# A linear-attention, expert-layer and feed-forward kernel: the attention's inverse products over 128 rows, and the constants and tables around them packed

## The chip, the cores and the metric

The kernel runs on one core of a Trainium2 chip. The core has five engines that work side by side: TensorE (PE, matrix products; its weight loads are listed apart as PEld), VectorE (DVE), ScalarE (ACT), GpSimd (POOL) and SyncE (SP, which here only issues transfers). Sixteen DMA engines move data between the chip's memory and the core's on-chip memory, SBUF; PE writes to a second on-chip memory, PSUM. [...] The metric is the time of one execution in microseconds (us) of the device; less is better.

## The reference

Three parts follow each other. A recurrence over 768 steps for 4 x 8 heads, each with a 40 x 40 state; a layer of eight experts, of which each of 3072 tokens takes two; and a feed-forward layer with leaky rectifier. All that is changed lies in the recurrence:

```python
def _attn_ref(r, k, v, w, a, b):
    state = np.zeros((B, H, D, D)); y = np.zeros_like(r)
    for t in range(S):
        ...
        y[:, :, t] = np.einsum('bhd,bhde->bhe', rt, state)
        Sa = np.einsum('bhde,bhe->bhd', state, at)
        state_decay = state * wt[:, :, None, :] - np.einsum('bhd,bhe->bhde', Sa, bt)
        state = state_decay + np.einsum('bhd,bhe->bhde', vt, kt)
```

## The kernel before

**Chunks.** The 768 steps are cut into 12 chunks of 64. Within a chunk the steps' mutual dependence is solved by blocks: a chunk falls into two blocks (blk) of 32 steps, each of two halves (h) of 16, and for each 16 steps the inverse of a small triangular matrix is kept. The 32 heads are split into two bands (f = 0, 1) of 16 each, and the 16 into four groups g of four (z).

**The scan over a chunk.** For each group g, `c_x` (lines 163 to 175) gathers right sides: products of the state S with aT and of VU with g, in line 167, go to PSUM tile bk, and two copies by ACT (line 175) put them into the tile x[g]. Only 16 rows of x are written for each band: rows 0 to 15 and 32 to 47 for an even chunk, 64 to 79 and 96 to 111 for an odd one (p0 is 64 for odd chunks). `c_u` (lines 176 to 182) multiplies them with the inverse: line 180 runs eight products of 32 output rows and 40 columns, from 64 rows of TT (the weights) and 64 rows of x:

```python
for f in range(2): nc.tensor.matmul(pu[32*f:32*f+n,z],TT[p0:p0+64,16*h:16*h+n,2*(4*g+z)+blk],x[p0:p0+64,z,f],...)
```

The profile shows each such product as two, 3072 in all. The weights of one product are 32 elements of TT, each 32 elements (128 bytes) behind the one before. ACT (line 182) copies the result into VU, from which the next `c_x` reads. After four rounds `c_s` (line 183) brings the state forward: products of kb with VU in line 189, then DVE in lines 191 and 194. The four groups and neighbouring chunks overlap on PE; `y_s` and `y_y` (lines 203 to 223: lines 207, 215 and 220 on PE) make the output of a chunk, and `logits` (line 340) the first step of the expert layer.

**Preparing a chunk.** `wq` (line 76) runs twice for each chunk and makes running products of the decays by two scans on DVE: Dt (line 82, backwards, with the constant tile cd, which holds 4096 in every 64th column) and Et (line 88, forwards, with ce, whose every 64th column is set in line 87). POOL multiplies aT by Et (line 93). `sta` and `stk_` stack operands, and a transposing DMA in line 107 turns each of them (at, kbt; rt, ut and sd are further ones); `ks` (line 122) multiplies kbt with at in line 129, and stores a part, ns, to memory as nd (line 134). For two chunks at a time, `t_load` (line 137) fetches nd into N (line 139) and sets the tile T to unit matrices, `t_step` (line 143) eliminates in 15 steps (two operations of line 148 each, on POOL; on DVE for chunk 0), and `t_fin` (line 149) transposes T by DVE into one of two tiles TT (line 151). Chunks 0 and 1 are alone, so that only one half of T and TT is filled for them.

**Tiles.** T is 128 x 32 x 32, of which 32 matrices of 16 x 16 use the left 16 of each 32 columns. The tile tm holds products of a step. TT is 128 x 48 x 32; its rows 16 to 31 are cleared at the start (line 250), since a product of half h reads 32 rows of it from row 16h.

**Order.** `run` (line 232) lists all steps with a due time (`at(k, f, ...)`) and emits them by it. The program is then placed by the framework's own scheduler, which works with estimated durations, so the order on an engine is fixed when the program is built, and can change over a long stretch when one instruction changes. All loads, stores and transposing DMAs of this stage stand in one queue, SP's.

Of the kernel before, what the change touches and what calls it, by code (L numbers as in the profile page):

```python
# [7 lines left out]
F32 = mybir.dt.float32  # L8
# [4 lines left out]
ALU = mybir.AluOpType  # L13
# [16 lines left out]
class Attn:  # L30
# [7 lines left out]
    def consts(s,tp):  # L38
        nc=s.nc; cp=s.cp; V=nc.vector; G=nc.gpsimd;

        s.S=cp.tile([128,16,120],F32,name="S"); G.memset(s.S,0.0)
        s.ss=cp.tile([128,16,128],F16,name="ss"); V.memset(s.ss,0.0)
        s.x=[cp.tile([128,4,2,40],F32,name=f"x{i}") for i in range(4)]
        for t in s.x: G.memset(t,0.0)
# [31 lines left out]
    def wq(s,c,q):  # L76
# [3 lines left out]
        def rv(t): b=t[:,n-1:n]; return bass.AP(tensor=b.tensor,offset=b.offset,ap=[b.ap[0],[-1,n]])  # L80
        w=s.K['w',c,q]; ws=w[:,1:513].rearrange("p (a b)->p a b",b=64); w0=s.w0[:,c,is_]
        V.tensor_tensor_scan(rv(f2(Dt)),rv(w[:,2:514]),rv(f2(s.cd)),0.0,ALU.mult,ALU.add)  # L82
        W4=wp.tile([104,8],F32,name="W4",bufs=2)
        V.tensor_copy(ws[:,:,0],w0); V.memset(ws[:,:,63],0.0)
        V.tensor_tensor(W4,w0,Dt[:,:,0],ALU.mult)
        V.tensor_scalar(w0,W4,2.0**-12,None,op0=ALU.mult)
        V.reciprocal(W4,W4); V.tensor_scalar(s.ce[:,:,0],W4,2.0**15,None,op0=ALU.mult)
        V.tensor_tensor_scan(f2(Et),w[:,0:512],f2(s.ce),0.0,ALU.mult,ALU.add)  # L88
        v=lambda t: t.rearrange("p z (o x)->p z o x",o=2)[:,:,:,0:40]
# [47 lines left out]
    def t_load(s,c):  # L137
        nc=s.nc; wk=s.wk; p=s.tp(c)
        nc.sync.dma_start(out=s.N[p].rearrange("p a b->p (a b)"),in_=s.K[c]['nd'][p])
        e=nc.gpsimd; e.memset(s.blk(c,s.T,0,[32,16],[1,16]),0.0); e.memset(s.blk(c,s.T,0,[33,16]),1.0)  # L140
    def blk(s,c,t,off,*d):
        x=t.rearrange("p a b->p (a b)")[s.tp(c),0:1]; return bass.AP(tensor=x.tensor,offset=x.offset+off,ap=[x.ap[0],[512+16*(t is s.N),2]]+[list(z) for z in d])
    def t_step(s,c,j):
        nc=s.nc; n,m=15-j,j+1; te=s.cfg['te0' if c==0 else 'te']
        e=nc.vector if te=='V' else nc.gpsimd
        t=s.tm[s.tp(c),0:2*n*m].rearrange("p (o a b)->p o a b",o=2,b=m)
        nd,T0,T1=s.blk(c,s.N,33*j+1,[1,n],[0,m]),s.blk(c,s.T,32*j,[0,n],[1,m]),s.blk(c,s.T,32*m,[32,n],[1,m])
        e.tensor_tensor(t,nd,T0,ALU.mult); e.tensor_tensor(T1,T1,t,ALU.subtract)
    def t_fin(s,c):
        s.nT+=1; TT=s.TT[s.nT%2]; p=s.tp(c); f2=lambda x: x.rearrange("p a b->p (a b)")  # L150
        for i in range(2): s.tlast=s.nc.vector.transpose(f2(TT[p,32*i:32*i+16]),f2(s.T[p,16*i:16*i+16]))
        for i in s.tg[c]: s.K[i]['TT']=TT
# [10 lines left out]
    def c_x(s,c,g,blk,h):  # L163
        nc=s.nc; K=s.K[c]; aT=s.aT[c%s.cfg['NA']]; VU=s.VU[c%2]; p0=64*(c%2); cs=slice(32*blk+16*h,32*blk+16*h+16); st=[True]*2
        px=s.bk[g]
        def mm(f,c0,n,l,r):
            q=64+32*f; nc.tensor.matmul(px[q:q+16,c0:c0+n],l,r,start=st[f],stop=True,skip_group_check=True); st[f]=False  # L167
        if c:
            for j in range(2):
                for f in range(2): i=4*g+2*j+f; mm(f,80*j,80,aT[:,i,cs],s.S[:,i,0:80])  # L170
        for z in range(4):
            for f in range(2): mm(f,40*z,40,K['g',f][:,4*g+z,cs],VU[:,f,4*g+z,:])
        x=s.x[g]
        for f in range(2):
            nc.scalar.activation(x[p0+32*f:p0+32*f+16,:,f],px[64+32*f:80+32*f,0:160].rearrange("p (z d)->p z d",d=40),AF.Copy,scale=-0.125)  # L175
    def c_u(s,c,g,blk,h):
        nc=s.nc; TT=s.K[c]['TT']; VU=s.VU[c%2]; p0=64*(c%2); x=s.x[g]; n=32
        pu=s.bk[g][:,0:160].rearrange("p (a d)->p a d",a=4)
        for z in range(4):
            for f in range(2): nc.tensor.matmul(pu[32*f:32*f+n,z],TT[p0:p0+64,16*h:16*h+n,2*(4*g+z)+blk],x[p0:p0+64,z,f],start=h==0 and z==0,stop=True,skip_group_check=True)  # L180
        for f in range(2):
            q=64-64*f+32*blk; nc.scalar.activation(VU[q:q+n,f,4*g:4*g+4],pu[32*f:32*f+n],AF.Copy)  # L182
# [49 lines left out]
    def run(s):  # L232
        nc=s.nc; F=s.cfg; s.st=s.P("ast"); s.wk=s.P("awk")
        s.pre=ExitStack(); s.wp=s.pre.enter_context(s.tc.tile_pool(name="awp",bufs=1)); s.ctx.enter_context(s.pre)
        V=nc.vector
        zero=lambda t: (nc.gpsimd if t.dtype==F32 else V).memset(t,0.0)
        s.w0=s.wk.tile([104,NCH,16],F32,name="w0"); nc.sync.dma_start(out=s.w0.rearrange("p a b->p (a b)"),in_=s.h['w0'])
        s.cd=s.wp.tile([104,8,64],F32,name="cd"); s.ce=s.wp.tile([104,8,64],F32,name="ce")
        zero(s.cd); zero(s.ce); V.memset(s.cd[:,:,63:64],4096.0)
        s.aT=[s.st.tile([128,16,64],F32,name=f"aT{i}") for i in range(F['NA'])]  # L240
# [5 lines left out]
        for t in s.VU: zero(t)  # L246
        s.T=s.wk.tile([128,32,32],F32,name="T",bufs=1); zero(s.T)
        s.N=s.wk.tile([128,32,32],F32,name="N",bufs=1); s.tm=s.wk.tile([128,272],F32,name="tmp",bufs=1)
        s.TT=[s.st.tile([128,48,32],F32,name=f"TT{i}") for i in range(2)]; s.nT=0
        for t in s.TT: zero(t[:,16:32])  # L250
        s.bk=[s.ps.tile([128,512],F32,name=f"bk{g}",bufs=1) for g in range(4)]
# [613 lines left out]
```

## Time and profile before

| | us |
|---|---|
| median of 3 runs (1504.52 to 1516.42) | 1512.85 |
| the profiled execution | 1518.96 |
| its span, from the first to the last instruction | 1517.2 |

| engine | busy us | share of the span | instructions |
|---|---|---|---|
| PE | 1207.4 | 80% | 15975 |
| PEld | 909.3 | 60% | 15975 |
| DVE | 892.2 | 59% | 2029 |
| ACT | 641.7 | 42% | 1535 |
| POOL | 482.7 | 32% | 559 |

The profile records one execution. A busy time is the time in which at least one instruction of the engine ran; PE's products overlap each other, so their starts and not their durations show the pace, and the ends are modelled. The chain of waits is followed back from the last instruction, at each step to what released it. [...] In the rows, `L180 PE MATMUL bk<-x,TT 64*32 64x40 f32 x16` is sixteen products of line 180 that write bk from x and TT, with 64 rows and 32 columns of weights, and 64 x 40 elements that run through.

### The profile page before, as it was taken

The page shows a single profiled execution, that of the slowest core. Times are in us where ns is not written, and L with a number is a line of the kernel's source. Part 1 is how long each engine was busy: PE and PEld are TensorE (multiplying, and loading weights), DVE is VectorE, ACT ScalarE, POOL GpSimd, SP SyncE. Part 2 cuts the span into 40 slices and gives each one's busy share as a digit, 9 for nine tenths or more (in the row PEclk, how much of TensorE's full clock was granted, in tenths as well). Part 3 has the DMA queues.
Part 4 walks back from the last instruction along what each step waited for, and adds up shares of the span by engine and source line. Part 5 has one row for each costly group of instructions (what it writes and reads, how often), then busy time and mean ns, then how long its engine had stood idle before and what let it go on. Part 6 is the DMA issues. An engine that isn't in the chain of part 4 may idle for free.

```text
span 1517.2 us, 37921 instructions
## 1 busy us (share of the span) xinstructions
PE 1207.4 (80%) x15975; PEld 909.3 (60%) x15975; DVE 892.2 (59%) x2029; ACT 641.7 (42%) x1535; POOL 482.7 (32%) x559
## 2 busy tenths in 40 slices
PE   1348877879788879627877978779895899999998
PEld 0237766768677768515646746547675565555555
DVE  6798655765666589674644554869732764442321
ACT  1247556565666755332422223325221544433432
POOL 7365414224152343132402102030003525423422
PEclk9999688885878977758999989889998899999999
DMA  7779787877867664559637766465312522110000
GB/s 216 142 139 196 139 157 145 151 128 157 157 129 142 120 141 107 104 176 177 165 107 204 205 208 180 121 194 138 119 44 82 109 66 48 35 36 18 18 18 21
DMA packets 305939, 188.17 MB, mean 124 GB/s; under 512 B 260894, under 2 KB 276355, under 8 KB 304891
## 3 DMA queue, kind: packets, MB, share of 16 engines
q1 hardware_dynamic: 293103, 156.91, 46.7%
q0 software_dynamic: 10368, 16.84, 4.4%
q10 hardware_dynamic: 2288, 11.90, 2.3%
q8 instruction: 127, 2.08, 0.6%
q14 instruction: 53, 0.43, 0.1%
HBM read 105.24 MB, written 23.18 MB: 85 GB/s over the span
## 4 chain that ended last, share of the span: by engine, by line
PE 49%; DVE 21%; DMA 18%; issue 4%; POOL 3%; ACT 3%; SPq 2%; another core or an unknown queue 1%; DVEq 0%; POOLq 0%; ACTq 0%
PE ph L661 10%; PE po L671 9%; PE po L565 9%; PE ph L551 7%; DMA wf<-w 7%; PE bk L167 5%; DMA kbt<-stk 3%; PE bk L180 3%; DVE l L520 2%; DVE S L194 2%; DVE kb L99 2%; DVE Dt L82 1%; DVE wam L510 1%; DVE Et L88 1%; DMA N<-nd 1%
## 5 line engine op out<-in xcount | busy, mean ns | idle before, releaser
L551 PE MATMUL ph<-xT,h 128*128 128x372 f16 (+2 forms) x680 | 151.6, 353 | 83.7 <-DVE gl L554 56.3
L553 ACT ACTIVATE gh<-ph 128x372 f16<-128x372 f32 (+2 forms) x136 | 68.1, 509 | 260.9 <-PE ph L551 221.6
L529 POOL DMA_INDIRECT xr<-xs,ix x56 | 82.9, 1480 | 254.8 <-DMA xT<-xr 234.5
L175 ACT ACTIVATE x<-bk 16x160 f32<-16x160 f32 x384 | 113.7, 296 | 94.8 <-PE bk L167 87.6
L551 PEld LDWEIGHTS <-h 128*128 128x128 f16 x680 | 68.5, 101 | 129.6 <-issue 93.5
L665 POOL TENSOR_TENSOR gl<-hc,gh 128x512 f16<-128x512 f32 x80 | 91.9, 1157 | 146.7 <-ACT gh L664 146.6
L565 PE MATMUL po<-h,gh 128*124 128x320 f16 x448 | 135.4, 303 | 0.6 <-ACT y L567 0.4
L565 PE MATMUL po<-l,gh 128*124 128x320 f16 x448 | 134.7, 303 | 0.0
L565 PE MATMUL po<-h,gl 128*124 128x320 f16 x448 | 134.2, 304 | 0.0
L180 PE MATMUL bk<-x,TT 64*32 64x40 f32 x3072 | 130.7, 244 | 2.5 <-issue 1.7
L661 PE MATMUL ph<-xT,wih 128*128 128x512 f16 (+2 forms) x560 | 125.2, 354 | 7.8 <-DVE hc L663 4.5
L167 PE MATMUL bk<-S,aT 128*16 128x80 f32 x1408 | 105.5, 276 | 31.0 <-DVE S L194 19.4
L565 PEld LDWEIGHTS <-gh 128*124 128x124 f16 x896 | 122.4, 137 | 10.2 <-issue 0.9
L182 ACT ACTIVATE VU<-bk 32x160 f32<-32x160 f32 x384 | 112.4, 293 | 35.9 <-PE bk L180 27.2
L167 PE MATMUL bk<-VU,g 128*16 128x40 f32 x3072 | 126.0, 230 | 1.7 <-ACT VU L182 1.7
L663 DVE SCALAR_TENSOR_TENSOR hc<-ph,hc 128x512 f32<-128x512 f32 (+2 forms) x112 | 68.4, 612 | 98.2 <-ACT hc L662 93.3
L180 PEld LDWEIGHTS bk<-x,TT 64*32 64x32 f32 x3072 | 109.7, 156 | 16.8 <-issue 5.0
L671 PE MATMUL po<-woh,gh 128*128 128x320 f16 x384 | 114.1, 301 | 5.0 <-issue 3.7
L671 PE MATMUL po<-wol,gh 128*128 128x320 f16 x384 | 113.8, 301 | 0.0
L639 POOL DMA_INDIRECT yy<-yd,slot x48 | 48.6, 1013 | 204.6 <-DMA yd<-y 157.5
L664 ACT ACTIVATE gh<-hc 128x512 f16<-128x512 f32 (+2 forms) x112 | 62.5, 566 | 119.5 <-PE po L671 66.6
L671 PE MATMUL po<-woh,gl 128*128 128x320 f16 x384 | 109.4, 301 | 0.1
(286 smaller groups left out, 2504.0 us busy)
## 6 DMA issues: line engine op xcount, KB each, us to landing
wf<-w SPq DMA_DIRECT2D x24, 512.0 KB
w<-wi SPq DMA_DIRECT2D x16, 768.0 KB
wf<-w SPq DMA_DIRECT2D x32, 320.0 KB
w<-wo SPq DMA_DIRECT2D x16, 640.0 KB
kb<-kb SPq DMA_DIRECT2D x24, 320.0 KB
yd<-y ACTq DMA_DIRECT2D x7, 1085.0 KB
w<-wz SPq DMA_DIRECT2D x24, 208.8 KB
aa<-aa SPq DMA_DIRECT2D x12, 320.0 KB
```

Source lines behind the costliest of these rows:

```text
L167: q=64+32*f; nc.tensor.matmul(px[q:q+16,c0:c0+n],l,r,start=st[f],stop=True,skip_group_check=True); st[f]=False
L175: nc.scalar.activation(x[p0+32*f:p0+32*f+16,:,f],px[64+32*f:80+32*f,0:160].rearrange("p (z d)->p z d",d=40),AF.Copy,scale=-0.125)
L180: for f in range(2): nc.tensor.matmul(pu[32*f:32*f+n,z],TT[p0:p0+64,16*h:16*h+n,2*(4*g+z)+blk],x[p0:p0+64,z,f],start=h==0 and z==0,stop=Tr ...
L182: q=64-64*f+32*blk; nc.scalar.activation(VU[q:q+n,f,4*g:4*g+4],pu[32*f:32*f+n],AF.Copy)
L529: c=e*NJ+j; nc.gpsimd.indirect_dma_start(out=xr[0:PT,j],out_offset=None,in_=s.xs,in_offset=bass.IndirectOffsetOnAxis(ap=s.ix[0:PT,c:c+1],a ...
L551: for n,(t,k,i) in enumerate(ps): nc.tensor.matmul(ph[:,0:N],w(t,k,f),xT[:,j0:j1,i,0:PT],start=n==0,stop=n==7)
L553: nc.scalar.activation(o,ph[:,0:N],AF.Relu)
L565: nc.tensor.matmul(po[0:PT,0:DM],a[:,f,c],b[:,DM*f:DM*f+DM],start=n==0,stop=n==23); n+=1
L661: for n,(t,k,i) in enumerate(ps): nc.tensor.matmul(ph[:,0:N],w(t,k,f),xT[:,b0:b1,i,:],start=n==0,stop=n==7)
L663: nc.vector.scalar_tensor_tensor(c,ph[:,0:N],0.01,c,ALU.mult,ALU.max)
L665: (nc.vector if g<2 else nc.gpsimd).tensor_tensor(gl[:,f,0:N],c,gh[:,f,0:N],ALU.subtract)
L671: nc.tensor.matmul(po[:,0:DM],a[:,f,128*(b-b0):128*(b-b0)+128],bb[:,f,:],start=n==0,stop=n==47); n+=1
```

## The change

Five edits go together.

1. There are eight tiles x in place of four: an odd chunk has its own. As all of them are cleared at the start and `c_x` writes the same rows as before, the rows of the other parity stay zero. The product of line 180 (182 now) runs over all 128 rows of TT and x.
2. Both tiles TT are cleared as a whole at the start.
3. T is packed: 33 x 16 columns in place of 32 x 32, so a row of a matrix stands 16 elements behind the one before, not 32. The transposition in `t_fin` still reads 32 columns for each row, of which the second 16 are now the next row; they end in rows of TT that meet zero rows of x.
4. The tile tm has 128 columns in place of 272.
5. The constant tile cd goes. ce has 520 columns and serves both scans: ahead of each Dt scan a memset on DVE puts 4096 into columns 64, 128, ... 512, and the Dt scan reads ce from column 1 on; ahead of the Et scan columns 0, 64, ... 448 are written as before.

```diff
@@ -40,7 +40,7 @@
-        s.x=[cp.tile([128,4,2,40],F32,name=f"x{i}") for i in range(4)]
+        s.x=[cp.tile([128,4,2,40],F32,name=f"x{i}") for i in range(8)]
         for t in s.x: G.memset(t,0.0)
@@ -79,13 +79,14 @@
-        V.tensor_tensor_scan(rv(f2(Dt)),rv(w[:,2:514]),rv(f2(s.cd)),0.0,ALU.mult,ALU.add)
+        ce=s.ce[:,0:512].rearrange('p (a b)->p a b',b=64)[:,:,0]; V.memset(bass.AP(tensor=s.ce[:,64:65].tensor,offset=s.ce[:,64:65].offset,ap=[s.ce[:,64:65].ap[0],[64,8]]),4096.0)
+        V.tensor_tensor_scan(rv(f2(Dt)),rv(w[:,2:514]),rv(s.ce[:,1:513]),0.0,ALU.mult,ALU.add)
         ...
-        V.reciprocal(W4,W4); V.tensor_scalar(s.ce[:,:,0],W4,2.0**15,None,op0=ALU.mult)
-        V.tensor_tensor_scan(f2(Et),w[:,0:512],f2(s.ce),0.0,ALU.mult,ALU.add)
+        V.reciprocal(W4,W4); V.tensor_scalar(ce,W4,2.0**15,None,op0=ALU.mult)
+        V.tensor_tensor_scan(f2(Et),w[:,0:512],s.ce[:,0:512],0.0,ALU.mult,ALU.add)
@@ -137,18 +138,19 @@
-        e=nc.gpsimd; e.memset(s.blk(c,s.T,0,[32,16],[1,16]),0.0); e.memset(s.blk(c,s.T,0,[33,16]),1.0)
+        e=nc.gpsimd; e.memset(s.blk(c,s.T,0,[16,16],[1,16]),0.0); e.memset(s.blk(c,s.T,0,[17,16]),1.0)
...
-        nd,T0,T1=s.blk(c,s.N,33*j+1,[1,n],[0,m]),s.blk(c,s.T,32*j,[0,n],[1,m]),s.blk(c,s.T,32*m,[32,n],[1,m])
+        nd,T0,T1=s.blk(c,s.N,33*j+1,[1,n],[0,m]),s.blk(c,s.T,16*j,[0,n],[1,m]),s.blk(c,s.T,16*m,[16,n],[1,m])
...
-        for i in range(2): s.tlast=s.nc.vector.transpose(f2(TT[p,32*i:32*i+16]),f2(s.T[p,16*i:16*i+16]))
+        for i in range(2):
+            t=s.T[p,16*i:16*i+1]; s.tlast=s.nc.vector.transpose(TT[p,32*i:32*i+16],bass.AP(tensor=t.tensor,offset=t.offset,ap=[t.ap[0],[16,16],[1,32]]))
@@ -170,14 +172,14 @@
-        x=s.x[g]
+        x=s.x[4*(c%2)+g]
...
-            for f in range(2): nc.tensor.matmul(pu[32*f:32*f+n,z],TT[p0:p0+64,16*h:16*h+n,2*(4*g+z)+blk],x[p0:p0+64,z,f],start=h==0 and z==0,stop=True,skip_group_check=True)
+            for f in range(2): nc.tensor.matmul(pu[32*f:32*f+n,z],TT[:,16*h:16*h+n,2*(4*g+z)+blk],x[:,z,f],start=h==0 and z==0,stop=True,skip_group_check=True)
@@ -235,8 +237,8 @@
-        s.cd=s.wp.tile([104,8,64],F32,name="cd"); s.ce=s.wp.tile([104,8,64],F32,name="ce")
-        zero(s.cd); zero(s.ce); V.memset(s.cd[:,:,63:64],4096.0)
+        s.ce=s.wp.tile([104,520],F32,name="ce")
+        zero(s.ce)
@@ -244,10 +246,10 @@
-        s.T=s.wk.tile([128,32,32],F32,name="T",bufs=1); zero(s.T)
-        s.N=s.wk.tile([128,32,32],F32,name="N",bufs=1); s.tm=s.wk.tile([128,272],F32,name="tmp",bufs=1)
+        s.T=s.wk.tile([128,33,16],F32,name="T",bufs=1); zero(s.T)
+        s.N=s.wk.tile([128,32,32],F32,name="N",bufs=1); s.tm=s.wk.tile([128,128],F32,name="tmp",bufs=1)
         s.TT=[s.st.tile([128,48,32],F32,name=f"TT{i}") for i in range(2)]; s.nT=0
-        for t in s.TT: zero(t[:,16:32])
+        for t in s.TT: zero(t)
```

The change also moves instructions on every engine, since the scheduler places the program anew. Up to line 82 the lines keep their numbers; line 167 becomes 169, 180 becomes 182, 220 becomes 222. Three places follow, before and after.

On PE, at the place that the profile before shows at 432 us: products of the scan (L167: right sides, L180: with the inverse, L189: state) and of the output (L220). The numbers behind bk, x and TT are those of buffers; an `x8` is the eight products of one `c_u`. Before:

```order
L167 MATMUL bk_195<-VU_96,g 16x40 x4
L180 MATMUL bk_196<-x_90,TT_190 32x40 x8
L180 MATMUL bk_193<-x_87,TT_190 32x40 x3
L220 MATMUL yy<-kb,s_6103 32x40 x16
L180 MATMUL bk_193<-x_87,TT_190 32x40 x5
L180 MATMUL bk_194<-x_88,TT_190 32x40 x8
L180 MATMUL bk_195<-x_89,TT_190 32x40 x8
L189 MATMUL bk_196<-VU_95,kb 40x40 x8
```

After:

```order
L169 MATMUL bk_200<-VU_104,g 16x40 x4
L182 MATMUL bk_201<-x_90,TT_195 32x40 x8
L182 MATMUL bk_198<-x_91,TT_195 32x40 x3
L222 MATMUL yy<-kb,s_6130 32x40 x16
L182 MATMUL bk_198<-x_91,TT_195 32x40 x5
L182 MATMUL bk_199<-x_92,TT_195 32x40 x8
L182 MATMUL bk_200<-x_93,TT_195 32x40 x8
L191 MATMUL bk_201<-VU_103,kb 40x40 x8
```

The sequence is the same here; line 182 reads tiles of even (x_87 to x_90) and of odd chunks (x_91 to x_94), so two chunks meet within one run of products, before as after.

In SP's queue, around the transposing DMA of at that the profile before shows at 188 us (aa is a load that at is made from, nd a store, VU, rr, w and kb loads). Before:

```order
L66 DMA w<-wz 104x514
L73 DMA aa<-aa 128x640
L74 DMA aT_161<-at 40x1024 x2
L66 DMA w<-wz 104x514
L107 DMA_TRANSPOSE at<-stk_176 128x16x128
L134 DMA nd<-ns 64x16x32
L107 DMA_TRANSPOSE kbt<-stk_177 128x16x128
L107 DMA_TRANSPOSE ut<-us 128x16x128
L161 DMA VU_96<-vv 64x640 x2
L155 DMA rr<-rr 128x640
L107 DMA_TRANSPOSE kbt<-stk_175 128x16x128
L134 DMA nd<-ns 64x16x32
```

After:

```order
L74 DMA aT_166<-at 40x1024 x2
L66 DMA w<-wz 104x514
L135 DMA nd<-ns 64x16x32
L108 DMA_TRANSPOSE ut<-us 128x16x128
L163 DMA VU_104<-vv 64x640 x2
L73 DMA aa<-aa 128x640
L108 DMA_TRANSPOSE at<-stk_181 128x16x128
L108 DMA_TRANSPOSE kbt<-stk_182 128x16x128
L66 DMA w<-wz 104x514
L157 DMA rr<-rr 128x640
L108 DMA_TRANSPOSE kbt<-stk_180 128x16x128
L135 DMA nd<-ns 64x16x32
```

The load of aa and the transposes of at and of the first kbt stood ahead of the transpose of ut and the loads of VU, and stand behind them now.

On POOL, at the end of the memsets of the start-up. Before:

```order
L236 MEMSET aT_163 32x1024 x2
L236 MEMSET aT_164 32x1024 x2
L236 MEMSET TT_189 128x512
L236 MEMSET TT_190 128x512
L93 TENSOR_TENSOR aT_160<-aT_160,Et 104x512 x2
L104 TENSOR_TENSOR stk_176<-aa,stk_176 128x16x40
```

After:

```order
L238 MEMSET aT_168 32x1024 x2
L238 MEMSET aT_169 32x1024 x2
L238 MEMSET TT_194 128x1536
L238 MEMSET TT_195 128x1536
L94 TENSOR_TENSOR aT_165<-aT_165,Et 104x512 x2
L105 TENSOR_TENSOR stk_181<-aa,stk_181 128x16x40
```

The two memsets of TT stand at the same place, between those of aT and the first product aT times Et, with 1536 columns in place of 512.

## Rows read from the trace of the kernel before

**Rows 1.** Busy time by stretch (from:to, length, each engine in us, granted clock, DMA share, GB/s).

```profile
98.00:634.00 536.00, 443.75 (x11065) 387.77 (x11067) 368.51 (x913) 325.55 (x953) 196.75 (x307) 0.81 0.73 141
367.10:367.90 0.80, 0.80 (x22) 0.71 (x22) 0.80 (x1) 0.60 (x3) 0.00 (x0) 0.50 0.47 98
432.30:435.10 2.80, 2.80 (x112) 2.65 (x109) 1.28 (x3) 2.07 (x6) 0.93 (x1) 1.00 1.15 188
```

**Rows 2.** The chain of waits from 98 to 634 us, share of it by line.

```profile
by line: PE bk L167 13.4%; DMA kbt<-stk 7.8%; PE bk L180 7.8%; issue 5.4%; DVE S L194 4.6%; DVE kb L99 3.3%; DMA ut<-us 2.7%; DMA nd<-ns 2.5%; DMA N<-nd 2.3%; DVE Dt L82 2.3%; PE pt L95 2.0%; DMA kb<-kb 1.9%; DVE stk L106 1.9%; PE sc L129 1
```

**Rows 3.** Page, costliest groups: L180 products, busy us, mean ns, idle before.

```profile
L180 PE MATMUL bk<-x,TT 64*32 64x40 f32 x3072 | 130.7, 244 | 2.5 <-issue 1.7
```

**Rows 4.** Timeline of PE near 432 us: start us, busy us, engine, line, operation, count.

```profile
432.02 0.34 PE L167 MATMUL bk<-VU,g 128*16 128x40 f32 x8
432.29 0.74 PE L180 MATMUL bk<-x,TT 64*32 64x40 f32 x22
432.96 0.49 PE L220 MATMUL yy<-kb,s 128*32 128x40 f32 x32
433.38 1.54 PE L180 MATMUL bk<-x,TT 64*32 64x40 f32 x42
434.85 0.53 PE L189 MATMUL bk<-VU,kb 128*40 128x40 f32 x16
```

**Rows 5.** One line each: duration of one in ns (min/median/max), first and last start.

```profile
L180 PEld LDWEIGHTS bk<-x,TT x3072: 128/158/173, 98.4 to 633.1; 64*32 64x32 f32 x192
L180 PE MATMUL bk<-x,TT x3072: 208/235/288, 98.4 to 633.2; 64*32 64x40 f32 x192
L220 PEld LDWEIGHTS yy<-kb,s x1536: 105/113/178, 139.9 to 648.1; 128*32 128x32 f32 x192
L220 PE MATMUL yy<-kb,s x1536: 199/207/277, 139.9 to 648.1; 128*32 128x40 f32 x192
```

**Rows 6.** Timeline of PE near 512 us, two lines of 128 rows.

```profile
511.80 0.35 PE L167 MATMUL bk<-VU,g 128*16 128x40 f32 x10
511.95 0.23 PE L220 MATMUL yy<-kb,s 128*32 128x40 f32 x2
```

**Rows 7.** Timeline of PE near 367 us, at half the clock.

```profile
366.41 0.75 PE L167 MATMUL bk<-VU,g 128*16 128x40 f32 x16
367.08 0.76 PE L180 MATMUL bk<-x,TT 64*32 64x40 f32 x16
367.78 0.45 PE L167 MATMUL bk<-S,aT 128*16 128x80 f32 x4
```

**Rows 8.** Timeline of PE near 508 us, L180 of two chunks in a run.

```profile
508.38 0.97 PE L180 MATMUL bk<-x,TT 64*32 64x40 f32 x32
```

**Rows 9.** The chain in the start-up: start us, us, what.

```profile
24.84 0.99 POOL TT L236 x2
25.83 1.24 POOL aT L93
```

**Rows 10.** POOL to 30 us by line: count, busy us, mean ns, idle before.

```profile
L236 POOL MEMSET aT<- 32x1024 f32 x10 | 9.4, 944 | 5.3 <-DVE bad L798 4.9
L41 POOL MEMSET S<- 128x1920 f32 x1 | 1.7, 1697 | 0.3 <-POOLq L858 0.3
L236 POOL MEMSET TT<- 128x512 f32 x2 | 1.0, 528 | 0.1
```

**Rows 11.** DVE, line L84: the memset of 104x8, ns min/median/max.

```profile
L84 DVE MEMSET w<- x24: 65/65/65, 11.4 to 462.4; 104x8 f32 x24
```

**Rows 12.** The chain near 166 us.

```profile
166.13 8.01 DMA ut<-us
```

**Rows 13.** Timelines of DVE and PE: the last TT, and its first product.

```profile
537.03 1.30 DVE L151 STREAM_TRANSPOSE TT<-T 128x512 f32<-128x512 f32 x2
547.88 0.30 PE L180 MATMUL bk<-x,TT 64*32 64x40 f32 x2
```

**Rows 14.** Line L167: idle time of PE before it, by what ended it.

```profile
  DVE S L194: 38.5, 21
```

More of the change, by code (lines that the diff above doesn't have):

```diff
@@ L139, in t_load @@
         nc.sync.dma_start(out=s.N[p].rearrange("p a b->p (a b)"),in_=s.K[c]['nd'][p])
-        e=nc.gpsimd; e.memset(s.blk(c,s.T,0,[32,16],[1,16]),0.0); e.memset(s.blk(c,s.T,0,[33,16]),1.0)
+        e=nc.gpsimd; e.memset(s.blk(c,s.T,0,[16,16],[1,16]),0.0); e.memset(s.blk(c,s.T,0,[17,16]),1.0)
     def blk(s,c,t,off,*d):
-        x=t.rearrange("p a b->p (a b)")[s.tp(c),0:1]; return bass.AP(tensor=x.tensor,offset=x.offset+off,ap=[x.ap[0],[512+16*(t is s.N),2]]+[list(z) for z in d])
+        x=t.rearrange("p a b->p (a b)")[s.tp(c),0:1]; return bass.AP(tensor=x.tensor,offset=x.offset+off,ap=[x.ap[0],[528 if t is s.N else 256,2]]+[list(z) for z in d])
     def t_step(s,c,j):
@@ L176, in c_u @@
     def c_u(s,c,g,blk,h):
-        nc=s.nc; TT=s.K[c]['TT']; VU=s.VU[c%2]; p0=64*(c%2); x=s.x[g]; n=32
+        nc=s.nc; TT=s.K[c]['TT']; VU=s.VU[c%2]; x=s.x[4*(c%2)+g]; n=32
         pu=s.bk[g][:,0:160].rearrange("p (a d)->p a d",a=4)
         for z in range(4):
-            for f in range(2): nc.tensor.matmul(pu[32*f:32*f+n,z],TT[p0:p0+64,16*h:16*h+n,2*(4*g+z)+blk],x[p0:p0+64,z,f],start=h==0 and z==0,stop=True,skip_group_check=True)
+            for f in range(2): nc.tensor.matmul(pu[32*f:32*f+n,z],TT[:,16*h:16*h+n,2*(4*g+z)+blk],x[:,z,f],start=h==0 and z==0,stop=True,skip_group_check=True)
         for f in range(2):
```

## The prediction

> **What bounds the kernel now.** The page's table gives shares over the whole span, and the span is made of unlike stages, so I read the busy times by stretch first: attention runs until 634 us, and all that is changed runs before that; the 883 us of expert and feed-forward stages behind it only shift. From 98 to 634 us no engine is full [rows 1]: TensorE (PE) is busy 444 of 536 us, VectorE (DVE) 369, ScalarE (ACT) 326, the DMA engines at 0.73, with a mean granted clock of 0.81. [...] Next I read the chain of waits through this stage, which is a mixture too: its largest entry, the products of L167, holds 13.4%, the transposing DMA of kbt 7.8%, the product with the inverse (L180) 7.8% [rows 2]. What L180 saves passes to the end only where L180 is on that chain: 7.8% of 536 us is 41.8 us, of 130.7 us that the line is busy [rows 3], or 0.32. The other bound is 444/536 = 0.83, which would hold if PE alone set the pace. I take 0.32, since that row is about this very line, and keep 0.83 for the range.
>
> **What L180 costs now.** Last come the single rows of PE. Two things stand in them. First, a change of the array's shape stops PE. Around 432 us, at the full clock [rows 1, 4], the last start of a row is its start plus its busy time less one product's duration (0.207 us for a 40-column product of 128 rows, 0.235 for L180, [rows 5]). So L167's last product starts at 432.15 and L180 follows at 432.29, 0.14 us later; L180 (22) starts its last at 432.80, L220 follows 0.16 later; L220 to L180 is 0.14; L180 to L189 is 0.16. L180 alone is 64 rows by 32 columns. L167 and L220 have 128 rows and at most 32 columns, and between these two there is no gap: at 511.80 ten products of L167 start their last at 511.94, and L220 starts at 511.95 [rows 6]. At half the clock [rows 1, 7] L180's 16 products (0.76, less some 0.26 for the last) start their last at 367.58 and L167 follows 0.20 later. With 62% at the full clock a boundary costs some 0.17 us, of which about 0.02, the ordinary step, is left where shapes agree: 0.15 saved.
>
> Second, within a run L180's products follow each other at (1.54-0.235)/41 = 32 ns at the full clock, L189's, with 128 rows and 40 columns, at (0.53-0.207)/15 = 21.5 [rows 4, 5]. At half the clock 16 products take 0.75 (L167) and 0.76 (L180), the same [rows 7]. So L180 hardly gains from the faster clock: something beside the array holds it. Its weight loads take 158 ns, those of L220, just as wide, 113 [rows 5]. L180's differ in two ways: 64 rows in place of 128, and weights read from TT with a step of 32 elements, where the others lie side by side. The change removes the first and keeps the second.
>
> **The change, part by part.** *Shape.* Counted over the order's rows, L180 stands in 157 runs before and 156 after. In the new order 114 of their 312 boundaries face L167 or L220 and become free: 114 x 0.15 = 17.1 us. Some 95 exits to other shapes fall from 0.16 to the 0.14 of entries, 1.9 us. Against it the new order changes shape more often elsewhere: 524 times in all, where the old order, counted as if L180 had 128 rows, has 491: 33 x 0.15 = 5.0 us. Net 14.0 us of PE time, of which 0.32, or 4.5 us, passes.
>
> *Pace within a run.* No row prices 128 rows with stepped weights. Bounds: nothing, if the step is the cause, and 3072 x 0.62 x (32-21.5) ns = 20 us of PE time, if the rows are. I take nothing: a pace that does not follow PE's clock [rows 4, 7] looks like reading memory, and the reading stays. [...]
>
> *What it loses.* With 64 rows, an even and an odd chunk can run side by side in the array. At 508.38 us 32 products of two chunks take 0.97 us [rows 8]; at 32 ns each they would take 31 x 0.032 + 0.235 = 1.23. So 0.26 us is gone where two chunks meet in a run; in the run of 22 at 432 us [rows 4], by the same working, 0.17. The old order has 23 such places: at 0.21 on average 4.8 us of PE time, 1.5 us on the path.
>
> *Start-up.* GpSimd (POOL) clears all of TT, 1536 columns in place of 512, twice. On the chain of the start these two stand between the memsets of aT and the first product of aT and Et, which frees Et for the second scan [rows 9]: no cover. 512 columns take 0.53 us and 1920 take 1.70 [rows 10], so 1536 take 1.38 and the two add 1.7 us. Four more tiles x (1280 columns) against the missing cd (512) and the smaller T (496) leave 272 columns, 0.2 us; they lie in front of POOL's wait of 4.9 us for DVE [rows 10], which covers them. Were that wait gone, they would cost the 0.2.
>
> *Scan constants.* 24 memsets of 104x8 come in on DVE at 65 ns [rows 11], some 90 with their issue, and one such goes. Behind each stand the scan Dt and what follows it. Eight are in the start-up, whose chain runs over these scans: 0.7 us in full. Of sixteen in the stage, 1.4 us, I take a third: 0.5. The bounds are nothing and 2.2. Scans alternated Dt, Et, Dt before, so sharing one tile adds no order. The packed T is read and written with as many elements as before, and its lead (below) covers it: nothing.
>
> *The order.* The scheduler has placed everything up to 634 us anew. No row prices that as a whole; I take zero, with two of the rivals as its bounds.
>
> Sum: -4.5 + 1.5 + 1.7 + 1.2 = -0.1 us. The profiled execution's own time is 1518.96 us, its span of 1517.2 and 1.8 around it; that is 0.4% above the median of 1512.85. The sum gives 1518.9 for it, and **1513** against the median: gain and loss cancel. With 0.83 in place of 0.32 the PE terms are -7.6 and the result is 1508.
>
> **The rivals.** *The rows were the cause (chance 0.22).* L180 then steps at 21.5 ns and 20 us more of PE time goes: 6.4 at 0.32, giving 1506.4; 16.6 at 0.83, which with the 1508 above gives 1491. For it: L180 alone has 64 rows, and it alone is slow. Against it: the equality at half the clock.
>
> *The new order delays the inverse (0.14), the slower side.* All loads and transposes stand in SP's one queue. In three places (near 188, 332 and 474 us of before) the load of aa and the transposes of at and kbt move behind nd, a transpose of ut and loads of VU; one transpose of ut has held the chain for 8.0 us [rows 12], so each preparation of a chunk comes about as much later. What covers it is the lead of TT: for the last pair it is written at 537.03 and first used at 547.88, 11 us [rows 13]. It decides once a move costs more than that lead, as two transposes in a row would: 5 us over, in three places, give 1513 + 15 to 18 = 1528 to 1531. Against it: one move alone is shorter than the lead.
>
> *The new order removes waits (0.14).* At L167 PE waits 38.5 us for S of L194 [rows 14]; an interleaving that halves this gives 1513 - 19 = 1494. Nothing in the rows says that it does.
>
> *The gaps come back as waits (0.10).* Products that start earlier wait for the same DMA or DVE row, the gain of PE vanishes: 1512.85 + 2.9 = 1516, inside the forecast's own range.
>
> **How the numbers follow.** The likeliest case has 0.40, with 1513 and its own range of 1508 to 1517. Faster by over 1% (under 1497.7; 1% is about what a measurement of this kernel can tell from no change) takes two fifths of the first rival, most of the lucky order: 0.21. Slower by over 1% (over 1528) takes most of the slow order and a remnant: 0.13. The rest is 0.66. A range that leaves out two tenths goes from 1496 to 1524: the lower end cuts the last part of the two faster cases, the upper end most of the slow one.
>
> **What would show it.** L180's products with 128 rows; steps of about 0.02 us between L167, L180 and L220 in the timeline; runs of L180 at 31 to 32 ns a product at the full clock (21 to 22 would be the first rival); the two TT memsets at 1.38 us each on the chain of the start; the stretch to 634 us within a few us of before. I am wrong if L180's share of the chain was no measure of what a saving passes on, or if the placing of the queues outweighs all of these terms.

## The result: 3% faster

The changed kernel takes 1467.74 us in the median of four runs (1465.06 to 1470.09), the kernel before beside it 1514.3 (1504.52 to 1516.42): a ratio of 0.971, 95% interval 0.967 to 0.975. The forecast was 1513, with a range of 1496 to 1524. The profiled execution of the changed kernel has a span of 1465.5 us.

Most of the gain lies where the change lies. The first product with the inverse starts at 101.1 us (98.4 before), the last at 588.2 (633.2): the stage between them shrank from 535 to 487 us, and what follows it took 877 us in place of 884. (These are two single executions, and the one of before lay 5 us over its median here; a64 below, which is no faster than before in the median, has 877 us there too.) The same stretch as in [rows 1], after the change (from:to, length, PE, PEld, DVE, ACT, POOL busy, granted clock, DMA share, GB/s):

```profile
101.00:588.20 487.20, 393.68 (x11082) 347.65 (x11085) 362.27 (x901) 325.48 (x951) 201.87 (x305) 0.88 0.80 155
```

TensorE is busy 50 us less, DVE 6 less, ACT as long as before; the granted clock of TensorE in these rows, as a share of the full one, rose from 0.81 to 0.88. PE's idle time in the stage is what it was, 93.5 us against 92. By line (busy us and mean ns of one, idle before), two lines from the page of after and then one from that of before:

```profile
L182 PE MATMUL bk<-x,TT 128*32 128x40 f32 x3072 | 135.3, 242 | 13.8 <-ACT x L177 7.2
L169 PE MATMUL bk<-VU,g 128*16 128x40 f32 x3072 | 110.8, 217 | 3.1 <-ACT VU L184 1.6
```

```profile
L167 PE MATMUL bk<-VU,g 128*16 128x40 f32 x3072 | 126.0, 230 | 1.7 <-ACT VU L182 1.7
```

The changed line, 130.7 us busy in [rows 3], did not get shorter. The untouched line 169 (167 before) did, from 126.0 us to 110.8. PE's waits in the stage, by us in total, times and longest; the longest before, then those of after:

```profile
PE bk L167 <- DVE S L194: 19.4, 11, 3.6
```

```profile
PE sc L130 <- DMA kbt<-stk: 13.1, 8, 3.2
PE yy L217 <- DVE xt L224: 9.8, 9, 3.3
PE ys L209 <- DMA ut<-us: 9.3, 6, 2.5
PE bk L169 <- ACT VU L184: 8.5, 12, 2.9
PE bk L182 <- ACT x L177: 7.2, 8, 1.9
...
PE bk L169 <- DVE S L196: 5.6, 7, 1.8
...
PE bk L182 <- DVE TT L153: 3.2, 3, 1.9
```

For S of DVE PE's products waited 19.4 us before, now 5.6. [rows 14] has 38.5 us for it because that row adds the waits of PE's weight loads, 19.1 us, to the products' own. Waits for xt and x have grown in its place, and three waits for TT are new. The start-up went as forecast: on its chain the two memsets of TT take 2.70 us where [rows 9] had 0.99, and the new memset of DVE takes the 65 ns of [rows 11].

```profile
25.99 2.70 POOL TT L238 x2
28.69 1.23 POOL aT L94
```

### The profile page after: what moved, and what is told of

Same layout as the page of the kernel before. It is cut to its first block, busy times and chain, and to the rows that moved or that the text cites. A ratio compares the mean times of both kernels' runs of the same rounds, so it can differ in the third digit from the quotient of the medians.

```text
span 1465.5 us, 37940 instructions
## 1 busy us (share of the span) xinstructions
PE 1155.6 (79%) x15975; PEld 866.7 (59%) x15975; DVE 893.8 (61%) x2052; ACT 642.4 (44%) x1535; POOL 489.6 (33%) x562
## 4 chain that ended last, share of the span: by engine, by line
PE 45%; DVE 22%; DMA 18%; issue 5%; POOL 4%; ACT 3%; SPq 2%; ACTq 0%; DVEq 0%; POOLq 0%
PE ph L663 10%; PE po L673 10%; PE po L567 8%; PE ph L553 6%; DMA wf<-w 6%; PE bk L169 4%; PE bk L182 2%; DMA kbt<-stk 2%; DVE l L522 2%; DVE kb L100 2%; DMA w<-wi 2%; DMA ut<-us 1%; DVE Dt L83 1%; DVE wam L512 1%; DVE Et L89 1%
## 5 line engine op out<-in xcount | busy, mean ns | idle before, releaser
L182 PE MATMUL bk<-x,TT 128*32 128x40 f32 x3072 | 135.3, 242 | 13.8 <-ACT x L177 7.2
L182 PEld LDWEIGHTS bk<-x,TT 128*32 128x32 f32 x3072 | 115.2, 160 | 26.7 <-ACT x L177 9.4
L184 ACT ACTIVATE VU<-bk 32x160 f32<-32x160 f32 x384 | 112.5, 293 | 38.4 <-PE bk L182 27.4
L567 PEld LDWEIGHTS <-gh 128*124 128x124 f16 x896 | 122.2, 137 | 10.1 <-ACT gh L555 1.1
L169 PE MATMUL bk<-VU,g 128*16 128x40 f32 x3072 | 110.8, 217 | 3.1 <-ACT VU L184 1.6
L512 DVE TENSOR_REDUCE wam<-wf 128x1 f32<-128x1024 f32 (+1 forms) x35 | 46.4, 1324 | 97.3 <-DMA wf<-w 96.9
```

Source lines behind the costliest of these rows:

```text
L182: for f in range(2): nc.tensor.matmul(pu[32*f:32*f+n,z],TT[:,16*h:16*h+n,2*(4*g+z)+blk],x[:,z,f],start=h==0 and z==0,stop=True,skip_group_ ...
L567: nc.tensor.matmul(po[0:PT,0:DM],a[:,f,c],b[:,DM*f:DM*f+DM],start=n==0,stop=n==23); n+=1
```

## The experiments: shape and order apart

Two things changed at once: the shape of the products, and the scheduler's order. **Theory A** puts the gain on the stops, the gaps that the prediction found where products of one tile shape follow those of another; **theory B** puts it on the order, **theory C** on the packing and the eight x tiles. The order can be held while the shape changes: the scheduler places the program for one shape, and then each product of line 182 is rewritten to the other, with no other instruction touched. The rewriting, in short:

```
for q in products_of_line_182:            # placed already
    ins = [first `rows` partitions from p0 of each operand]
    q = replace(q, ins=ins, tile_size=(rows, 32), tile_position=(p0 if rows == 64 else 0, col))
```

**a64**: eight tiles, packing and all else of the change, but 64 rows, scheduled as such (`TT[p0:p0+64,...]`, `x[p0:p0+64,z,f]` in line 182). Its order is close to that of before: 89% of TensorE's weight loads belong to the same line at the same place of the sequence, in the changed kernel 54%.

> The changed kernel with the products of line 182 on the 64 rows of their own chunk, scheduled as such: eight zero-padded x tiles, packed T, tm and scan constants, but no 128-row product. Theories A and B: like before and 2 us for the longer start, 1513 to 1517 us. Theory C (packing or eight x tiles): 1468 us.

Measured: 1506.1 us, 0.998 of before (0.9955 to 1.0008). Packing and tiles together are worth nothing that can be told. C falls.

**order_a64_128**: the order of a64, rewritten to 128 rows.

> The other corner: the changed kernel's tiles and packing with the order that the scheduler makes when the products are on 64 rows (close to the order before), and then each product run over all 128 rows. Theory A (shape): 1468 to 1480 us, most of the gain without the new order. Theory B (order): 1505 to 1515 us. My prediction's share of 0.32 for 14 us of stops would give 1509. If the granted clock of the stage rises from 0.81 without the new order, the clock follows from the stops.

Measured: 1493.0 us, 0.990 (0.987 to 0.993): 13 us under a64 with every instruction at its place.

**order_after_64**: the order of the changed kernel, rewritten to 64 rows.

> Every instruction of the changed kernel in the changed kernel's order, but each product of line 182 reads only the 64 rows of its own chunk, as before. In this order TensorE enters the inverse's products about 359 times against 157 before, so there are more changes of tile shape than before. Theory A (the stops at a change of shape were the cost, and they pass on in full): the 14.0 us that I counted for 157 entries become about 32, so about 1500 us, 30 over the changed kernel. Theory B (the scheduler's other order alone makes the gain): about 1468 to 1476 us. Theory C (packing the scan constants and the inverse, or the eight x tiles, made the gain): 1468 us.

Measured: 1481.5 us, 0.982 (0.977 to 0.988). So neither A nor B has all of it: at 64 rows the order alone takes 24 us off a64 (0.998 to 0.982), and the shape 14 to 17 us more. Theory A was priced too high for this kernel: the 359 entries into line 182 come from the trace of the changed kernel, where products of neighbouring lines start in between each other. With 64 rows and the same instructions they do not, and the trace has 155 entries (a64 152, and order_a64_128, with the instructions of a64, 339). The stage in a64, order_a64_128 and order_after_64, columns as above:

```profile
100.70:628.40 527.70, 441.77 (x11042) 386.53 (x11042) 368.29 (x924) 325.64 (x951) 194.15 (x305) 0.81 0.71 143
```

```profile
100.90:614.50 513.60, 402.35 (x11042) 354.78 (x11042) 368.50 (x924) 325.86 (x951) 195.09 (x305) 0.86 0.75 146
```

```profile
100.90:599.80 498.90, 431.63 (x11079) 377.27 (x11079) 363.34 (x901) 325.51 (x951) 200.60 (x305) 0.84 0.76 151
```

Down the shape (first to second, third to after): PE's busy time falls by 39.4 and 37.9 us and the stage by 14.1 and 11.7; the clock in the rows rises by 0.05 and 0.04; PE's idle time grows by 25 and 26. Down the order (first to third): the stage falls by 28.8 us, of which PE's busy time holds only 10; its idle time falls from 86 to 67.

**Does the order follow from 128 rows, or is it a draw?** Theory D: the order is better because it was planned for 128 rows. Theory E: it is one draw of the scheduler among many. Two constants of the planner are moved a little, each with products on 128 and on 64 rows, and each is scheduled anew:

```
la_128, la_64:   la=3.2  ->  la=3.25
pb_128, pb_64:   pb=.5   ->  pb=.45
```

> The changed kernel with one planner constant moved (a chunk's preparation starts 3.25 instead of 3.2 chunks ahead), which changes the scheduler's order in 4746 of TensorE's rows. Theory D (the order is better because the products are planned on 128 rows): near the changed kernel, 1462 to 1475 us. Theory E (the order's 25 us are the luck of one draw of the scheduler, and only the 13 us of the shape come from the rows): anywhere from 1460 to 1500 us, likelier back towards 1493, where the order made for 64 rows stood with 128-row products.

> The same constant at 3.25 in the variant with 64-row products in the changed kernel's tiles (3080 of TensorE's rows in other places). Theory D: 1500 to 1512 us, as with 3.2 (1506). Theory E: 1475 to 1515 us, the spread of a draw.

> The changed kernel with another planner constant moved (the extra distance between pairs of chunks, 0.45 instead of 0.5), 4466 of TensorE's rows in other places. Theory D: 1462 to 1475 us. Theory E: 1460 to 1500 us.

> The same constant at 0.45 with 64-row products (4444 of TensorE's rows in other places). Theory D: 1500 to 1512 us, some 38 us over the 128-row kernel with the same constant. Theory E: 1475 to 1515 us, and the mean over the three settings of the constants is only about 13 us over that of the 128-row kernels.

Measured: la_128 0.987 (0.981 to 0.992), la_64 0.996 (0.993 to 0.999), pb_128 0.984 (0.979 to 0.989), pb_64 0.990 (0.987 to 0.994). D as stated falls: moving one constant by 2% takes some 20 us off the gain of the changed kernel, and of four orders with 128-row products its own is the best, by 16 to 28 us. E's ranges hold, but its second sign does not: the three kernels with 64-row products stand some 21 us over those with 128 in the mean, not 13. That planning for 128 rows helps by a few us in the mean is thus not excluded; three draws of each do not tell.

**Is the shape's worth a property of two orders?** The two new orders made for 128 rows, rewritten to 64:

> The order of the 128-row kernel with the constant at 3.25 (1486 us), products on 64 rows again. If the shape's worth is a property of the runs' edges (118 to 192 ns at each): 12 to 15 us slower, about 1499 us, TensorE's busy time in the stage up by about 38 us from 400 and the stage's time at the low clock up by 60 to 70 us from 138. If the 13 us belonged to the two orders tried: anything else.

> The order of the 128-row kernel with the constant at 0.45 (1484 us), products on 64 rows again. Property of the edges: about 1497 us, TensorE busy 445 instead of 407 us in the stage. Property of two orders: anything else.

Measured: 0.990 (0.988 to 0.992) and 0.993 (0.991 to 0.996), against 0.987 and 0.984 of the same orders with 128 rows. (With products on 64 rows the first two of the three orders made for 128 are 24 and 9 us faster than the same settings planned for 64, the third 5 us slower.) The stages, first la on 64 and on 128 rows, then pb:

```profile
100.80:619.90 519.10, 435.22 (x11042) 382.15 (x11042) 365.55 (x924) 325.31 (x951) 202.23 (x305) 0.83 0.74 145
```

```profile
100.70:607.10 506.40, 400.38 (x11040) 352.88 (x11042) 366.68 (x924) 325.54 (x951) 203.08 (x305) 0.88 0.77 149
```

```profile
100.90:623.80 522.90, 452.33 (x11030) 397.98 (x11032) 362.85 (x927) 326.48 (x951) 199.99 (x307) 0.80 0.74 144
```

```profile
101.00:609.20 508.20, 406.96 (x11030) 359.20 (x11032) 362.91 (x927) 326.43 (x951) 200.86 (x307) 0.85 0.76 148
```

In four orders the shape takes 14.1, 11.7, 12.7 and 14.7 us off the stage (mean 13.3) and 39.4, 37.9, 34.8 and 45.4 off PE's busy time (mean 39.4): 0.34 of it passes to the end of the stage. Each stage is one execution's, and those of order_after_64 and la_128 were the fastest of their four, 7 and 6 us under the median, so it is partly luck that the four lie so close. In whole times (differences of the ratios, by 1510 us) the four are 13, 14 to 17, 5 and 15 us, 12 in the mean, each with 6 to 10 us of uncertainty either way; the 5 of la alone, where 12 to 15 were expected, can't be told from nothing.

**Where 39 us of PE come from.** The clock records of before and after hold two levels alone, 0.50 and 1.00: 204.5 and 297.0 us of the stage before, 115.5 and 368.6 us of it after. I sorted the trace's products of each pair by line and by the granted clock at their start, and split the difference into busy time of one product at the same level and products that changed level. At the same level it is 17.9, 17.7, 17.1 and 18.0 us; the move from the lower level to the full one is 21.5, 20.3, 17.7 and 27.4 us. Stretches without a clock record are counted as low here, as in the times at the low clock that expectations name: line 169's products of 40 columns last 266 ns in them (a64, mean), 267 at the recorded low level and 202 at the full one. The low level so counted holds 231, 188, 205 and 250 us of the four stages with 64 rows, and 159, 118, 138 and 170 with 128. The clock in the rows counts such stretches as full. (Counted as full, 22 to 26 us would be at the same level, and 12 to 20 the move.) The page shows the gain on line 169, which the rewriting does not touch, here a64 and then order_a64_128:

```profile
L169 PE MATMUL bk<-VU,g 128*16 128x40 f32 x3072 | 126.6, 231 | 0.7 <-ACT VU L184 0.7
L169 PE MATMUL bk<-S,aT 128*16 128x80 f32 x1408 | 103.5, 274 | 25.2 <-DVE S L196 18.3
```

```profile
L169 PE MATMUL bk<-S,aT 128*16 128x80 f32 x1408 | 97.1, 261 | 32.8 <-DVE S L196 22.0
L169 PE MATMUL bk<-VU,g 128*16 128x40 f32 x3072 | 119.2, 222 | 2.0 <-ACT VU L184 1.4
```

Together 230.1 and 216.3 us: this line's own busy time falls by 13.8 us.

**Declared tile or rows?** In two kernels of the changed kernel's order the products of even chunks read 64 rows. tile_only declares them in a tile of 128 by 32 all the same, even_64 in one of 64 by 32:

```
tile_only:  ins = 64 rows,  tile_size = (128, 32)
even_64:    ins = 64 rows,  tile_size = (64, 32)
```

> The changed kernel in its own order; the products of the even chunks read only their own 64 rows, but are still declared in a tile of 128 rows by 32 columns. If the stop comes with the declared tile: the gaps on entering these runs stay as after the change, and the time is that of the changed kernel, about 1468 us. If it comes with the rows that a product reads (or if the rows themselves hold the clock up): the gaps and the lower granted clock come back for half of the products, about 1475 us, as in the next kernel.

> As the kernel before this one, with the same 64 rows for the even chunks, but declared in a tile of 64 by 32, which is what products on 64 rows get by themselves. Both readings of the stop expect half of the shape's 13 us back: 1474 to 1476 us, and the time at the low clock in the stage between 118 and 188 us (about 155).

Measured, beside after_again below: tile_only 0.976 (0.972 to 0.979), even_64 0.979 (0.976 to 0.983), after_again 0.973 (0.970 to 0.977). The times lean the way that the declared tile says, but their intervals overlap; the traces decide. PE near the same work in order_after_64 (64 by 32), then in tile_only (start us, busy us):

```profile
438.56 0.46 PE L169 MATMUL bk<-VU,g 128*16 128x40 f32 x16
438.94 1.57 PE L182 MATMUL bk<-x,TT 64*32 64x40 f32 x48
440.45 0.46 PE L169 MATMUL bk<-S,aT 128*16 128x80 f32 x8
```

```profile
430.44 0.35 PE L169 MATMUL bk<-VU,g 128*16 128x40 f32 x10
430.62 0.26 PE L182 MATMUL bk<-x,TT 64*32 64x40 f32 x1
430.62 0.20 PE L169 MATMUL bk<-VU,g 128*16 128x40 f32 x1
430.62 0.26 PE L182 MATMUL bk<-x,TT 64*32 64x40 f32 x1
430.63 0.27 PE L169 MATMUL bk<-VU,g 128*16 128x40 f32 x5
430.70 1.72 PE L182 MATMUL bk<-x,TT 64*32 64x40 f32 x46
```

In the first, by the prediction's working, line 169 starts its last product at 438.56 + 0.46 - 0.20 = 438.82 and line 182 follows 0.12 us later; back to line 169 it is 0.17. In the second, 64-row products start among those of line 169, 0.00 to 0.01 us apart. The stage, tile_only and even_64:

```profile
100.80:587.30 486.50, 399.28 (x11079) 352.17 (x11081) 360.94 (x901) 325.37 (x951) 201.62 (x305) 0.87 0.79 155
```

```profile
101.70:594.70 493.00, 419.38 (x11082) 368.07 (x11085) 358.61 (x901) 325.37 (x951) 202.03 (x305) 0.87 0.76 153
```

PE is busy 20 us longer with the small tile, about half of the 38 of all chunks, and the stage 6.5. By the split above 10.0 us are at the same level and 10.1 from products that changed level, though both rows show a mean clock of 0.87: with the stretches without a record the low level holds 138 us in tile_only and 172 in even_64. So the stop, and the clock that goes with it, come from the declared tile; rows read have no part that this pair shows.

**What limits a run of line 182.** flat stores the transposed inverse so that a product's 32 weights lie side by side; the order is the changed kernel's.

```
-  s.TT=[... [128,48,32] ...]      TT[:,16*h:16*h+n,2*(4*g+z)+blk]
+  s.TT=[... [128,32,48] ...]      TT[:,2*(4*g+z)+blk,16*h:16*h+n]
```

> The changed kernel with the same order of instructions, but the transposed inverse laid out so that the 32 weights of one product lie side by side in a row instead of 32 elements apart. If the step between weights binds the pace inside a run (two products in 65 ns at the full clock, as in both kernels): about 40 ns, so some 37 us less of TensorE's time in the stage, and by the share that passes on 1431 (all of it) to 1456 us (0.32 of it). If the row count or the drain of the products binds instead: no change in the pace, 1468 us.

> The changed kernel once more, on the same chip as the two forms beside it: 0.97 of before, about 1466 us.

> The layout with the weights side by side once more, against the changed kernel on the same chip. In its first run TensorE was busy 18 us less in the stage and the stage 2 us shorter. If TensorE's saved time passes on with the share that the shape showed (about 0.35): 6 us under the changed kernel. If what is saved inside a run is waited for instead: within 3 us of it.

Measured: 0.973 (0.968 to 0.978) at first; then, side by side, after_again 1466.5 us and flat_again 1469.5 us, 0.973 and 0.976 (0.972 to 0.980). Line 182 in after_again and in flat_again, ns min/median/max of products and of weight loads:

```profile
L182 PE MATMUL bk<-x,TT x3072: 196/237/291, 101.0 to 591.6; 128*32 128x40 f32 x192
...
L182 PEld LDWEIGHTS bk<-x,TT x3072: 131/162/177, 100.9 to 591.6; 128*32 128x32 f32 x192
```

```profile
L182 PE MATMUL bk<-x,TT x3072: 196/202/277, 101.2 to 591.9; 128*32 128x40 f32 x192
...
L182 PEld LDWEIGHTS bk<-x,TT x3072: 106/113/172, 101.2 to 591.9; 128*32 128x32 f32 x192
```

The load falls from 162 to 113 ns, and two products that took 65 ns (median, full clock) take 36. At the low level they take 67 in both. Line 182 is busy 101.9 us in flat and in flat_again, in place of 135.3 and 135.8. And the kernel is no faster, where 1431 to 1456 us had been expected. The stages, after_again and flat_again:

```profile
101.00:591.60 490.60, 396.48 (x11079) 349.78 (x11081) 363.41 (x901) 326.11 (x951) 202.38 (x305) 0.88 0.78 153
```

```profile
101.20:591.90 490.70, 376.45 (x11079) 323.56 (x11081) 366.83 (x901) 326.06 (x951) 201.48 (x305) 0.85 0.79 153
```

The 33 us are the line's own busy time, in part of which products of other lines ran too; PE as a whole is busy 20 us less. By the split above it is 26 us less at the same level and 6 us more for products that moved to the low level, which holds 149 us of the stage in place of 129. And these 20 turn into idle time whole. flat has a price of its own: DVE's transposes into TT, written with a step now, take 1.03 us in place of 0.68 (after_again and flat_again):

```profile
L153 DVE STREAM_TRANSPOSE TT<-T x14: 661/684/711, 100.1 to 506.0; 128x512 f32<-128x512 f32 x10, 64x512 f32<-64x512 f32 x4
```

```profile
L153 DVE STREAM_TRANSPOSE TT<-T x14: 1005/1028/1070, 100.0 to 506.1; 128x512 f32<-128x512 f32 x10, 64x512 f32<-64x512 f32 x4
```

On the chain of waits behind 102 us they hold 4.8 us in place of 2.0. With the shape's share of 0.34, 20 us less of PE and 3 us more of TT make -4 us; measured are 3 to 5 more, with some 8 of uncertainty either way. So whether time saved inside a run passes less than time saved at a stop is not decided. The chain through the stage says where the time went (shares by line, after_again and flat_again):

```profile
by line: PE bk L169 10.5%; issue 8.8%; DMA kbt<-stk 7.8%; PE bk L182 6.9%; DMA ut<-us 5.6%; DVE kb L100 3.0%; POOL T L149 2.6%; DMA sd<-ss 2.5%; POOL tmp L149 2.3%; DVE Dt L83 2.3%; ACT VU L184 2.1%; DVE stk L107 2.0%; DMA N<-nd 1.9%; DVE s
```

```profile
by line: PE bk L169 10.8%; issue 9.4%; DMA kbt<-stk 6.8%; DMA ut<-us 4.0%; DMA N<-nd 3.8%; ACT VU L184 3.4%; PE bk L182 3.3%; ACT x L177 3.0%; POOL T L149 2.9%; DMA kb<-xd 2.7%; POOL tmp L149 2.4%; DMA sd<-ss 2.3%; DVE Dt L83 2.3%; DVE kb L
```

Line 182 loses 3.6% of the chain, 18 us; ACT's evictions of VU and x (now 3.4 and 3.0%) and the inverse's load of N (1.9 to 3.8%) stand in its place. In the order of a64 it is the same:

> The order made for 64 rows with 128-row products (1493 us) and the weights side by side, so TensorE works about 20 us less in the stage, as between the changed kernel and its flat form. If the share of TensorE's time that passes on is about a third in this order: 1486 us. If work saved inside these runs is waited for in any order: 1490 to 1496 us.

Measured: 0.990 (0.987 to 0.993), where order_a64_128 had 0.990. PE's busy time in the stage fell by 12.8 us, from 402.35, by the split 25 us less at the same level and 13 more for products that moved to the low one:

```profile
101.10:618.00 516.90, 389.60 (x11042) 338.06 (x11042) 371.06 (x924) 325.46 (x951) 194.72 (x305) 0.81 0.74 145
```

No kernel of the study beats the changed one.

## Why the prediction was wrong, step by step

- **Start-up: right.** 1.7 us for TT and 0.7 for the memsets were forecast; the first product came 2.7 us later, 1.7 of it in TT's row.
- **Pace within a run: right.** The step of the weights is the cause, not the rows: with 128 rows line 182 kept its pace, two products in 65 ns at the full clock (63 before), and with the weights side by side it ran at 36. So the first rival falls. The weight loads go the same way: with 128 rows 162 ns (median) with the step and 113 without it; with the step 158 ns for 64 rows (before, and order_after_64) and 162 for 128. That such a pace "looks like reading memory" was the author's guess: the runs vary the step alone, and none shows by what it costs.
- **Shape: right in kind, mis-sized in PE's time.** "Net 14.0 us of PE time, of which 0.32, or 4.5 us, passes": measured are 39.4 us of PE time, of which 0.34, or 13.3 us, passes. At equal clock the stops are 17 to 18 us, near the 14.0 (in a held order the prediction's own terms are 17.1 + 1.9, less 4.8 for chunks that no longer run side by side, worked out from the 0.97 us of [rows 8]: 14.2). What the term left out is the clock: with the stops gone, products move from the lower level to the full one, 18 to 27 us more. I had held the clock of [rows 1] fixed, and had read it too high. The 62% at the full clock, used in the 0.15 us of a boundary and in the 20 us of the first rival, reads that row's 0.81 as a mix of 0.50 and 1.00. No run shows this share: 33 us at the start of that stage have no clock record, and L167's products of 40 columns last 265 ns in them (mean), as at the low level (266; 202 at the full one), so the full one held 297 of 535 us, 56%. With 56% the same working gives 0.17 us a boundary as before, and 18 us for the rival. That the share of 0.32 came out is luck as far as shown: it was read for time saved in L180, and much of the 39 us was saved at line 169.
- **Order: the step that failed most.** "I take zero." No row stood behind that zero. This order is worth 24 to 28 us at either shape (a64 to order_after_64 0.998 to 0.982, order_a64_128 to the changed kernel 0.990 to 0.973 or 0.971). That the scheduler gave this one is luck: la_128 and pb_128 got worse ones. The rival "the new order removes waits" named the sign, with 0.14 and 19 us, but its price was half of the 38.5 us that count the weight loads too; half of the products' 19.4 is 10. With 128 rows in both orders PE's wait for S falls from 22.0 to 5.6 us, with 64 from 18.3 to 5.2. Line 169's idle time in order_a64_128:

```profile
  DVE S L196: 22.0, 11
  ACT VU L184: 12.1, 16
```

  In la_128, 20 to 24 us slower than the changed kernel, it stands between:

```profile
  DVE S L196: 11.1, 11
  ACT VU L184: 8.3, 13
```

  That S is the cause is not shown: no run moves this wait alone, and on 64 rows la_64 waits 8.2 us for S at line 169 where a64 waits 18.3, and its stage is as long, 527.6 against 527.7 us. Shown is that the order as a whole carries some 25 us, and that a small push to the planner loses most of them.
- **The slow order: not here. The gaps that come back: in large part.** PE waits 9.3 us for ut in six places, the longest 2.5; none cost the 5 us that the slower rival needed. The lead of TT did shrink, from 11 us in [rows 13] to nothing: the last TT is written at 504.54 and PE waits 1.90 us for it: the TT came 32 us earlier than before, PE's first product with it 43 us earlier.

```profile
505.31 1.79 PE L182 MATMUL bk<-x,TT 128*32 128x40 f32 x49 [1.90 <-DVE TT L153]
```

  The last rival had the shape's gain come back as waits. Of the 39 us of PE's time that the shape saved 26 did, as idle time; of the 20 in flat all did, in part through its slower transposes.
- **Not isolated.** The 0.5 us for the scan memsets in the stage lie within a64's 0.998, and the 1.5 us for chunks that no longer run side by side within the shape's worth; no run takes either alone. The 90 ns of a scan memset with its issue were the author's estimate: a memset of 104x8 takes 65 ns in before and after, and two small rows of DVE in before (L87, 38.13 to 38.16 us) stand 30 ns apart.

In whole times the path from before over a64 and order_after_64 to the changed kernel goes -3, -24 and -14 to -17 us, the start-up's loss of 2.3 (the first product of a64 comes at 100.7) among the first: -41 to -44 in all.

## What to carry to other kernels

Where a trace shows that a change of tile shape stops TensorE (here 0.12 to 0.17 us from start to start) in a stage whose granted clock is under full (here 0.80 to 0.84 with 64 rows), price the stop twice: once for the gap, once for the products around it that then run at the other level; here the second, 18 to 27 us, was as large as the first, 17 to 18. Look also whether clock records cover the stage before you trust its mean clock. Before crediting a change with its gain, hold the scheduler's order and rewrite the instruction alone, and move a planner's constant to see how wide the orders scatter: here over some 25 us, twice the worth of the shape itself. Busy time saved on an engine is not time saved: of the shape's 39 us 0.34 passed on, and of a pace 1.8 times as fast inside line 182's runs nothing that could be measured, since the clock, longer transposes and waits took it.

## What the runs showed that was not expected

- The stop comes with the declared tile, not with the rows read: 64-row products declared as 128 by 32 start 0.00 to 0.01 us from those of other lines, and declared as 64 by 32 0.12 to 0.17 us.
- Line 182's products declared as 128 by 32 and the 128-row products of other lines that stand next to them in the program start in between each other: the same instructions enter line 182 152 times in a64 and 339 times in order_a64_128. So entries counted in such a trace are not stops.
- A faster engine lost clock: with two products of line 182 in 36 ns in place of 65, the low level held 149 us of the stage in place of 129, in the other order 196 in place of 159, and gave back 6 of 26 us and 13 of 25.
- Moving the step from the weights to the transposes that write them made these 1.03 us long in place of 0.68, and the whole no faster.
- Why 39 us of stops and clock pass on a third stays open, and so does whether the 13 to 20 us saved inside the runs pass less. The chain shows ACT and the load of N in place of line 182 in flat; a run that isolates the clock's part was not made.
